# Ten rows of the last but one V tile, loaded by GpSimd on chosen DMA engines

## Chip, cores and metric

The kernel runs on one core of a Trainium2 chip. The metric is device time in microseconds (us): the median over the runs shown, and for the profile the span of one profiled execution. The core has five engines: TensorE (PE in the profile, its weight loads PEld), VectorE (DVE), ScalarE (ACT), GpSimd (POOL) and SyncE (SP). Data comes from the chip's memory (HBM) into the on-chip SBUF through 16 DMA engines that work beside them.

## What is computed

One decode step: attention of a single query over a cache of 65,536 keys and values for 8 key/value heads (16 query heads, head size 256), and a small gated feed-forward block, mixed by a sigmoid gate.

```
x = A_x                                        # 1 x 448
g = sigmoid((x * gate_w).sum(-1))
q = (x @ wq) as 16 heads of 256
scores = q . k_cache * 256**-0.5               # 8 kv heads x 65536 x 256, bf16
p = softmax(scores)
a = (p . v_cache) as 1 x 4096, then @ wo
gate, up = B_x @ W_gate, B_x @ W_up            # 448 x 1792 each
b = (relu(gate) * up) @ W_down
out = g * a + (1 - g) * b
```

The K and V caches are 268 MB each in bf16 and every byte of them is read once.

## The kernel before

**Tiles.** A K or V cache of a head is cut into four tiles, 32 K tiles and 32 V tiles in all. A tile is 128 partitions of 128 rows (U = 128) of 256 bf16 values: 64 KB in each partition, 8 MB in all. Three such buffers exist in SBUF, `ring[0]` to `ring[2]`. V tile 30 is the last but one (NT - 2 in the code, NT = 32), and it goes into `ring[1]`. V tile 31 is loaded in three pieces, `PIECES` = rows 0 to 64, 64 to 112 and 112 to 128, into `ring[2]`.

**Partitions of a V tile.** `v_src(n)` views a tile in memory as 32 groups of 4 partitions. Group p stands in partitions 4p to 4p + 3 of the buffer, so groups 16 to 31 are partitions 64 to 127.

**Order of the loads.** All large loads are issued by SP in the order of the list `order` (L381 to L394): K and V tiles by turns, then V tiles 28 to 31, then the output weights `wo` in six pieces of falling size (`WO`). A load waits until the last reader of its buffer has finished: for V tile 30 that reader is the product with V tile 28 (`free(("v", 30))`). What SP has issued waits in a queue at the DMA engines and is worked off in order.

**The work on a V tile.** `make_pv` writes two kinds of operation. ACT first copies the probabilities of the tile into `pcur` (L591), and this copy waits for the tile's load; only V tile 31 has the wait on its matmuls instead. Then 64 matmuls (L584) add the product to the accumulator `O`. After V tile 31, DVE scales the accumulator (L607 and L610), PE gathers it (L557), DVE copies it to `attnA` (L789), and 64 matmuls with `wo` (L551) follow, piece by piece as `wo` lands. Two casts (L796 and L797) and a store (L798) end the kernel.

**Numbers of a plan.** Each operation has a key, a planned time, and stands in its engine's program in the order of the keys; what it waits for is semaphores (`emit`, L89). A DMA adds 16 to its semaphore, and an operation that depends on several DMAs of one semaphore waits for their total.

**GpSimd** makes a few constants at the start (L443 to L461) and issues no load.

Of the kernel before, what the change touches and what calls it, by code (L numbers as in the profile page):

```python
# [27 lines left out]
class _Plan:  # L28
# [14 lines left out]
    def dma(self, eng, key, sem, fn, deps=()):  # L43
        if sem not in self.dsem:
            self.dsem[sem] = self.es.enter_context(self.nc.semaphore("d_" + sem))
        o = _Op(eng, key, fn, deps, dma=sem)
        self.ops.append(o)
        return o
# [212 lines left out]
def bass_gated_mix__gqa_block_cached__glu_gated_reglu__decode_kernel(  # L261
# [15 lines left out]
    DH = A_k_cache.shape[3]  # L277
# [4 lines left out]
    U = 128  # L282
    TK = 128 * U
    NTH = S // TK
    NT = H * NTH
# [11 lines left out]
    with es:  # L297
# [3 lines left out]
        ring = [sb("ring%d" % i, [128, U * DH], BF) for i in range(NRING)]  # L301
# [3 lines left out]
        scr = sb("scr", [128, 1024], BF)  # L305
        xcur = sb("xcur", [128, 136], BF)
        xm = sb("xm", [128, H * 128 + 8], BF)
# [63 lines left out]
        op, dma = pl.op, pl.dma  # L371
# [17 lines left out]
        for i, (lo, hi) in enumerate(PIECES):  # L389
            order.append(("vp", i, TILE * (hi - lo) / U))  # L390

        WO = [(0, 11), (11, 18), (18, 23), (23, 27), (27, 30), (30, 32)]
        for i, (lo, hi) in enumerate(WO):
            order.append(("wo", i, 0.27 * (hi - lo)))  # L394
        t = 3.0
        tL, issue = {}, []
# [16 lines left out]
        for kind, i, _ in order:  # L413
            if kind in ("k", "v") or (kind, i) in (("wo", 0), ("vp", 0)):
                r = place(kind, i)
# [105 lines left out]
        def v_src(i):  # L521
            h, a = divmod(i, NTH)
            return A_v_cache[0, h, :, :].rearrange("(t g p u) d -> g p t (u d)", t=NTH, g=NTH, u=U)[a]
# [37 lines left out]
        l_, qk, smax, aexp, pv, pc, last, first = {}, {}, {}, {}, {}, {}, {}, {}  # L561
        pending = []

        def free(key):
            out_ = []
            for f in freed[key]:
                out_.append(l_[f] if isinstance(f, str) else qk[f[1], 1] if f[0] == "k" else pv[f[1]])
            return out_
# [6 lines left out]
        def make_pv(n, lo, hi, sl, tv, dep):  # L575
            h, a = divmod(n, NTH)

            def f_pv(lo, hi):
                return lambda e: f_mm(e, lo, hi)

            def f_mm(e, lo, hi):
                for k in range(lo // 2, hi // 2):
                    g = k % 4
                    ins = e.matmul(OP[32 * g:32 * g + 4, :], pcur[a % 2][:, 4 * k:4 * k + 4],  # L584
                                   ring[sl][:, k * 512:(k + 1) * 512],
                                   start=False, stop=False, skip_group_check=True,
                                   tile_position=(0, 32 * g))
                return ins
            tp = max(tv, last["tev", h])
            if lo == 0:  # L590
                pc[n] = op("ap", max(tp - 5, last["tev", h] - 0.5), lambda e: e.copy(  # L591
                    pcur[a % 2][:].rearrange("p (k i) -> p k i", i=4),
                    ptp[:].rearrange("p (k i f) -> p k i f", i=4, f=4)[:, :, :, a]), last["ev", h] + [pv.get(n - 2)])
            if lo == 0 and a == 0:
                zero_o(last["tev", h] - 0.3, h)
            if n < NT - 1:
                pc[n].deps.append(dep)
            deps = ([dep] if n == NT - 1 else []) + [pc[n]] + ([last["zo", h]] if a == 0 and lo == 0 else [])
            if n >= NT - NTH and a == 1:
                for q_, (l2, h2) in enumerate(PIECES):  # L600
                    pv[n] = op("pv", tp + 0.1 * q_, f_pv(l2, h2), deps if q_ == 0 else [pc[n]], tag=("tail", 1, q_))
            else:
                tag = ("pv", a % 2, sl) if n < NT - NTH else ("tail", a % 2, 0 if n < NT - 1 else [q_[0] for q_ in PIECES].index(lo))
                pv[n] = op("pv", tp, f_pv(lo, hi), deps, tag=tag)
            if a == NTH - 1 and hi == U:
                tn = last["T", h + 1] + 18.5 if n < NT - 1 else tp + 1.2
                o1 = op("dx", tn, lambda e: e.tensor_scalar(o_sb[:], OP[:, 0:256], rcm[:, 0:1], None, ALU.mult),  # L607
                        [pv[n], last.get(("otr", h - 1)), last["rc", h]])
                last["ocp", h] = o1
                o1 = op("dx", tn + 0.05, lambda e: e.scalar_tensor_tensor(  # L610
                    o_sb[:], OP[:, 256:512], rcm[:, 1:2], o_sb[:], ALU.mult, ALU.add), [o1, last.get(("ec", h))])

                if h < H - 1:
                    o2 = op("pv", tn + 0.3, lambda e: f_sel(e, lambda d_: ecur[:, 7 - d_:135 - d_]),
                            [o1], tag="otr")
                else:
                    o2 = op("pv", tn + 0.5, lambda e: f_sel(e, lambda d_: esel[:, 120 - 16 * h - d_:248 - 16 * h - d_]),
                            [o1, g_es, l_["axz"]])
                if h < H - 1:
                    last["l5", h + 1].deps.append(o1)  # L620
                last["o1", h], last["otr", h] = o1, o2
                last["tn", h] = tn + 1

        for kind, i, t in sorted(issue, key=lambda q: q[0] != "wq"):
# [51 lines left out]
            elif kind == "k":  # L676
                n = i
                h, t_ = divmod(n, NTH)
                sl = slot["k", n]
# [28 lines left out]
                if t_ == NTH - 1:  # L708
# [18 lines left out]
                    for rd in range(2):  # L727
# [10 lines left out]
                        p = op("pe", tt + 0.5, f_ptr, [rsc, g_idb], tag=("ptr", rd))  # L738
# [29 lines left out]
            elif kind in ("v", "vp"):  # L768
                if kind == "v":
                    n, lo, hi = i, 0, U  # L770
                    sl = slot["v", n]
                    dep = dma("sp", t, "r%d" % sl, lambda e, sl=sl, n=n: e.dma_start(ring[sl][:], v_src(n)), free(("v", n)))
                else:
                    n, (lo, hi) = NT - 1, PIECES[i]
                    sl = slot["vp", 0]
                    dep = dma("sp", t, ("wq", "wqh", "wd")[i], lambda e, sl=sl, n=n, lo=lo, hi=hi: e.dma_start(  # L776
                        ring[sl][:, lo * 256:hi * 256], v_src(n)[:, :, lo * 256:hi * 256]), free(("vp", 0)))
                args = (n, lo, hi, sl, tL[kind, i], dep)
                if ("tev", n // NTH) in last:
                    make_pv(*args)  # L780
                else:
                    pending.append(args)
            elif kind == "wo":
                lo, hi = WO[i]
                l_["wo", i] = dma("sp", t, "wo%d" % i, lambda e, lo=lo, hi=hi: e.dma_start(  # L785
                    wo_sb[:, lo:hi, :], A_wo.rearrange("(p s) n -> p s n", s=32)[:, lo:hi, :]), free(("wo", 0)))

        LAST = last["tn", H - 1]
        aA = op("dx", LAST + 0.3, lambda e: e.tensor_copy(attnA[:], AX_ps), [last["otr", H - 1]])  # L789
        for i, (lo, hi) in enumerate(WO):  # L790
            def f_wo(e, lo=lo, hi=hi):
# [84 lines left out]
```

## Time and profile before

| what | before |
|---|---|
| device time, median of 3 runs | 1275.81 us (1275.78 to 1275.91) |
| span of the profiled execution | 1274.3 us |
| bytes read | 549.03 MB |
| PE busy | 365.9 us (29%) |
| DVE busy | 630.1 us (49%) |
| ACT busy | 78.0 us (6%) |
| POOL busy | 4.6 us (0%) |

The span runs from the first to the last instruction of the profiled execution. The device time has 1.5 us more in it. The profile has a page with the busy time of each engine, the DMA queues and the chain of work that ended last, and views that answer questions on the trace: a timeline of instructions, groups by line, busy time and DMA share in chosen stretches. Times in them are us from the start of the span.

### The profile page before, as it was taken

To read this page: it belongs to the slowest core of one execution; us is meant where nothing else is said; L and a number is where in the kernel's file an instruction comes from. 1 tells how busy PE (TensorE), PEld (TensorE's weight loads), DVE (VectorE), ACT (ScalarE), POOL (GpSimd) and SP (SyncE) were. 2 spreads that over 40 slices of the span, in tenths; PEclk is the share of its full clock that TensorE was granted. 3 is DMA by queue.
4 is the path that set the end of the run, shared out by engine and by line. 5 is a ranking of instruction groups with operands and counts; after the bars stand their busy time and mean duration, and the time that the engine had idled before them with its cause. 6 is when DMAs were issued, how large, how long until landed. Compare 5 with 4: busy or idle time off the path is not lost.

```text
span 1274.3 us, 10240 instructions
## 1 busy us (share of the span) xinstructions
PE 365.9 (29%) x4497; PEld 151.4 (12%) x4505; DVE 630.1 (49%) x309; ACT 78.0 (6%) x163; POOL 4.6 (0%) x23
## 2 busy tenths in 40 slices
PE   0534321133320332312233222323302332112525
PEld 0101110011110111101111110111100111001201
DVE  4777655553455633557433565335654355553300
ACT  0001100010000100001000010000000010000100
POOL 1000000000000000000000000000000000000000
PEclk9766665666655666656666656666566666566667
DMA  9999999999999999999999999999999999999998
GB/s 411 430 436 432 426 430 434 432 443 432 430 432 432 434 442 430 430 434 430 438 438 430 430 434 430 440 438 428 430 434 430 444 434 428 430 436 430 442 421 369
DMA packets 11389, 549.13 MB, mean 431 GB/s; under 512 B 1267, under 2 KB 1654, under 8 KB 2294
## 3 DMA queue, kind: packets, MB, share of 16 engines
q1 hardware_dynamic: 11378, 549.03, 99.7%
q8 instruction: 4, 0.07, 0.0%
q14 instruction: 3, 0.02, 0.0%
q10 hardware_dynamic: 4, 0.00, 0.0%
HBM read 549.03 MB, written 0.00 MB: 431 GB/s over the span
## 4 chain that ended last, share of the span: by engine, by line
DMA 81%; PE 16%; DVE 2%; ACT 1%; issue 1%; SPq 0%; ACTq 0%
DMA ring<-in_A_v_cache_dram 74%; PE O L584 13%; DMA ring<-in_A_wo_dram 3%; DMA ring<-in_A_wq_dram 2%; DMA ring<-in_A_k_cache_dram 2%; DVE ring L529 1%; PE ST L540 1%; ACT pcur L591 1%; PE O L501 1%; PE A_ps L551 0%; SPq L785 0%; SPq L776 0%; PE O L653 0%; DVE ring L660 0%; PE A_ps L653 0%
## 5 line engine op out<-in xcount | busy, mean ns | idle before, releaser
L529 DVE STREAM_TRANSPOSE ring<-ring 128x4096 uint32<-128x4096 uint32 x128 | 557.6, 4413 | 196.9 <-DMA ring<-in_A_k_cache_dram 196.9
L584 PE MATMUL O<-ring,pcur 128*4 128x512 bf16 x2048 | 187.3, 545 | 790.4 <-ACT pcur L591 781.9
L703 DVE TENSOR_REDUCE nmb<-ST 128x1 f32<-128x512 f32 x32 | 22.1, 692 | 345.9 <-PE ST L540 345.9
L584 PEld LDWEIGHTS O<-ring,pcur 128*4 128x4 bf16 x2048 | 59.3, 111 | 914.8 <-ACT pcur L591 794.6
L540 PE MATMUL ST<-ring,xcur 128*16 128x512 bf16 x2048 | 136.7, 420 | 44.3 <-DVE ring L529 43.7
L540 PEld LDWEIGHTS ST<-ring,xcur 128*16 128x16 bf16 x2048 | 62.4, 92 | 112.1 <-DVE ring L529 48.6
L705 ACT ACTIVATE P_sb<-ST,nmb 128x512 bf16<-128x512 f32 x32 | 44.6, 1392 | 368.3 <-DVE nmb L703 368.3
L591 ACT COPY pcur<-ptp 128x256 bf16<-128x256 bf16 x32 | 13.2, 415 | 732.6 <-DMA ring<-in_A_v_cache_dram 732.6
L607 DVE TENSOR_SCALAR o_sb<-O,rcm 128x256 bf16<-128x256 f32 x8 | 3.8, 479 | 61.1 <-PE O L584 61.1
L730 DVE TENSOR_TENSOR P_sb<-P_sb,hs 128x1024 bf16<-128x1024 bf16 x16 | 18.9, 1222 | 8.1 <-ACT hs L724 8.1
L735 PE MATMUL PT<-identb,P_sb 128*128 128x128 bf16 x128 | 14.5, 282 | 17.6 <-DVE P_sb L730 17.3
L501 PE MATMUL O<-ring,P_sb 128*128 128x512 bf16 x28 | 8.5, 477 | 17.3 <-DMA ring<-in_A_wq_dram 17.3
L735 PEld LDWEIGHTS PT<-identb,P_sb 128*128 128x128 bf16 x128 | 10.7, 127 | 19.9 <-DVE P_sb L730 19.9
L744 ACT COPY ptp<-PT 128x256 bf16<-128x256 bf16 x32 | 10.3, 375 | 23.0 <-PE PT L735 23.0
L705 ACT ACTIVATION_READ_ACCUMULATOR P_sb<-ST,nmb 128x1 f32 x32 | 8.3, 258 | 0.0
L501 PEld LDWEIGHTS O<-ring,P_sb 128*128 128x128 bf16 x28 | 3.2, 117 | 22.2 <-issue 20.5
L551 PE MATMUL A_ps<-ring,attnA 128*1 128x224 bf16 x64 | 5.3, 322 | 1.1 <-DMA ring<-in_A_wo_dram 1.0
L719 PE MATMUL M_ps<-identf,hs 128*2 128x128 f32 x8 | 2.3, 283 | 10.0 <-DVE hs L717 10.0
L756 DVE RECIPROCAL rc<-M_ps 128x2 f32<-128x2 f32 x8 | 1.4, 171 | 7.5 <-PE M_ps L755 7.5
L755 PE MATMUL M_ps<-hs,ones_f 128*128 128x2 f32 x16 | 4.5, 352 | 0.0
L722 PE MATMUL M_ps<-mx,nselT 2*128 2x1 f32 x16 | 3.2, 268 | 3.0 <-DVE mx L721 3.0
L755 PEld LDWEIGHTS M_ps<-hs,ones_f 128*128 128x128 f32 x16 | 4.0, 311 | 0.0
(93 smaller groups left out, 68.6 us busy)
## 6 DMA issues: line engine op xcount, KB each, us to landing
ring<-in_A_v_cache_dram SPq DMA_DIRECT2D x1, 4096.0 KB, 22.1
ring<-in_A_wq_dram SPq DMA_DIRECT2D x1, 3072.0 KB, 28.9
ring<-in_A_v_cache_dram SPq DMA_DIRECT2D x1, 3072.0 KB, 28.8
ring<-in_B_W_down_dram SPq DMA_DIRECT2D x1, 1568.0 KB, 53.0
ring<-in_B_W_gate_dram SPq DMA_DIRECT2D x1, 1344.0 KB, 26.3
ring<-in_B_W_up_dram SPq DMA_DIRECT2D x1, 1344.0 KB, 29.2
ring<-in_A_wo_dram SPq DMA_DIRECT2D x1, 1232.0 KB, 33.0
ring<-in_A_v_cache_dram SPq DMA_DIRECT2D x1, 1024.0 KB, 30.7
```

The costliest lines, as they stand in the source:

```text
L501: ins = e.matmul(QN_ps, xw3[:, kt, 31 - m:159 - m], rhs, start=(kt == 0 and m == 0), stop=(kt == R3 and m == J // 4 - 1))
L529: return lambda e: e.transpose(v, v)
L540: ins = e.matmul(bank[32 * w:32 * w + 16, :], xcur[:, x0:x0 + 16], ktv[sl][:, u0:u0 + 16, c, :, r_], start=(b == 0 and c == 0 and r_ == 0) ...
L551: ins = e.matmul(A_ps[32 * g:32 * g + 1, 0:D2], lhsT, rhs[:, g * D2:(g + 1) * D2], start=start, stop=stop, skip_group_check=True, tile_pos ...
L584: ins = e.matmul(OP[32 * g:32 * g + 4, :], pcur[a % 2][:, 4 * k:4 * k + 4], ring[sl][:, k * 512:(k + 1) * 512], start=False, stop=False, s ...
L591: pc[n] = op("ap", max(tp - 5, last["tev", h] - 0.5), lambda e: e.copy(pcur[a % 2][:].rearrange("p (k i) -> p k i", i=4), ptp[:].rearrange ...
L703: smax[n] = op("dv", sx, lambda e, n=n, t_=t_: e.tensor_reduce(NM[:, t_:t_ + 1], ST[n % 2][:], AX.X, ALU.max, negate=True), [qk[n, 1], las ...
L705: aexp[n] = op("ac", sx + 1, lambda e, n=n, t_=t_: e.activation(P_sb[:, t_:2048:4], ST[n % 2][:], ACTF.Exp, bias=NM[:, t_:t_ + 1], scale=1 ...
L730: rsc = op("dv", tt, lambda e, pb=pb: e.tensor_tensor(pb, pb, X[:, 12:16].unsqueeze(1).to_broadcast([128, 256, 4]), ALU.mult), [h7, aexp[n]])
L735: ins = e.transpose(PT[rd][:, s * 128:(s + 1) * 128], P_sb[:, (rd * 8 + s) * 128:(rd * 8 + s + 1) * 128], identb[:, :])
L744: ins = e.copy(dst, src)
L755: l3 = mop("pe", T + 19, lambda e: e.matmul(LS_ps, ones_f[:, :], X[:, 6:8], start=True, stop=True), [l2, c_one], tag="l3")
```

## The change

SP loads V tile 30 without part of it: first rows 0 to 117 of all 128 partitions, then rows 118 to 127 (`UW` = 10 rows) of partitions 0 to 63. The ten rows of partitions 64 to 127 are loaded by GpSimd. The table `WINDOWS` lists eight transfers, each as a flag and a number of groups. Four of them carry the tile's data, 3, 6, 2 and 5 groups of 4 partitions, 16 groups in all. Between them and after the last stand four tiny loads of 4, 2, 7 and 3 rows with two pieces of 64 bytes each, from `B_W_gate` into the scratch tile `scr`, whose content nobody reads afterwards. The eight numbers add up to 32, twice the number of DMA engines. All eight use the semaphore `vw`. ACT's copy for V tile 30 waits for `vw` as well, which is why a list of dependencies takes the place of the single one in `make_pv`.

```diff
+        UW = 10
+        WINDOWS = [(0, 3), (1, 4), (0, 6), (1, 2), (0, 2), (1, 7), (0, 5), (1, 3)]
...
-                pc[n].deps.append(dep)
-            deps = ([dep] if n == NT - 1 else []) + [pc[n]] + ([last["zo", h]] if a == 0 and lo == 0 else [])
+                pc[n].deps.extend(dep)
+            deps = (dep if n == NT - 1 else []) + [pc[n]] + ([last["zo", h]] if a == 0 and lo == 0 else [])
...
-                    dep = dma("sp", t, "r%d" % sl, lambda e, sl=sl, n=n: e.dma_start(ring[sl][:], v_src(n)), free(("v", n)))
+                    if n == NT - 2:
+                        part = lambda sl, n, p0, p1, u0, u1: dict(
+                            out=ring[sl][4 * p0:4 * p1, u0 * DH:u1 * DH], in_=v_src(n)[p0:p1, :, u0 * DH:u1 * DH])
+                        us = U - UW
+                        dma("sp", t, "r%d" % sl, lambda e, sl=sl, n=n: e.dma_start(**part(sl, n, 0, 32, 0, us)), free(("v", n)))
+                        dep = dma("sp", t + 0.01, "r%d" % sl, lambda e, sl=sl, n=n: e.dma_start(**part(sl, n, 0, 16, us, U)), free(("v", n)))
+                        p0 = 16
+                        for j, (skip, k) in enumerate(WINDOWS):
+                            if skip:
+                                seg = lambda a: a.rearrange("p (s w) -> p s w", s=2)[:, :, 0:32]
+                                sw = dma("gp", t + 0.02 + 0.01 * j, "vw", lambda e, k=k, j=j: e.dma_start(
+                                    seg(scr[16 * j:16 * j + k, 0:320]), seg(B_W_gate[0:k, 0:320])), [l_["xm"]] + free(("v", n)))
+                            else:
+                                sw = dma("gp", t + 0.02 + 0.01 * j, "vw", lambda e, sl=sl, n=n, p0=p0, k=k: e.dma_start(
+                                    **part(sl, n, p0, p0 + k, us, U)), free(("v", n)))
+                                p0 += k
+                        assert p0 == 32
+                    else:
+                        dep = dma("sp", t, "r%d" % sl, lambda e, sl=sl, n=n: e.dma_start(ring[sl][:], v_src(n)), free(("v", n)))
...
-                args = (n, lo, hi, sl, tL[kind, i], dep)
+                args = (n, lo, hi, sl, tL[kind, i], [dep] + ([sw] if (kind, i) == ("v", NT - 2) else []))
```

SP's program near its end before the change, with the semaphores that a load waits for in brackets. The two loads with `s_pe` are V tiles 28 and 29, the next is V tile 30, then come the three pieces of V tile 31 and the first two of `wo`:

```order
L772 DMA ring<-in_A_v_cache_dram 128x1x32768 [waits s_pe] x2
L772 DMA ring<-in_A_v_cache_dram 128x1x32768 [waits s_pv]
L776 DMA ring<-in_A_v_cache_dram 128x1x16384 [waits s_pv]
L776 DMA ring<-in_A_v_cache_dram 128x1x12288
L776 DMA ring<-in_A_v_cache_dram 128x1x4096
L785 DMA ring<-in_A_wo_dram 128x4928
L785 DMA ring<-in_A_wo_dram 128x3136
```

And with the change:

```order
L792 DMA ring<-in_A_v_cache_dram 128x1x32768 [waits s_pe] x2
L778 DMA ring<-in_A_v_cache_dram 128x1x30208 [waits s_pv]
L779 DMA ring<-in_A_v_cache_dram 64x1x2560
L796 DMA ring<-in_A_v_cache_dram 128x1x16384 [waits s_pv]
L796 DMA ring<-in_A_v_cache_dram 128x1x12288
L796 DMA ring<-in_A_v_cache_dram 128x1x4096
L805 DMA ring<-in_A_wo_dram 128x4928
L805 DMA ring<-in_A_wo_dram 128x3136
```

V tile 30 is now two loads of SP in the place of one; the order of all others is the same.

GpSimd's program with the change, from its last two constants to its end. Before, the branch at the end followed the constants:

```order
L462 TENSOR_SCALAR selc<-selc 128x2 [waits s_gp]
L463 TENSOR_SCALAR selc<-selc 128x2 [waits s_gp]
L787 DMA ring<-in_A_v_cache_dram 12x1x2560 [waits s_pv]
L784 DMA scr<-in_B_W_gate_dram 4x2x32 [waits s_dx]
L787 DMA ring<-in_A_v_cache_dram 24x1x2560
L784 DMA scr<-in_B_W_gate_dram 2x2x32
L787 DMA ring<-in_A_v_cache_dram 8x1x2560
L784 DMA scr<-in_B_W_gate_dram 7x2x32
L787 DMA ring<-in_A_v_cache_dram 20x1x2560
L784 DMA scr<-in_B_W_gate_dram 3x2x32
L828 UNCONDITIONAL_BRANCH
```

Eight loads are added, the first of them behind the same wait that V tile 30 has on SP.

ACT's program at its end with the change. The four copies at L593 are those of V tiles 28 to 31:

```order
L593 COPY pcur<-ptp 128x256 [waits d_r1,s_pv,s_ac]
L593 COPY pcur<-ptp 128x256 [waits d_r2,s_pv]
L593 COPY pcur<-ptp 128x256 [waits d_vw,d_r1,s_pv]
L593 COPY pcur<-ptp 128x256 [waits s_pv]
L817 CAST P_sb<-A_ps 1x224 [waits s_pv]
```

Only the third row differs: the copy for V tile 30 waits for `d_vw` too. The programs of PE and DVE are the same as before.

## The prediction

> **What bounds the kernel now.** I read the page first: the DMA lines, the queues and the chain that ended last.
>
> ```profile
> DMA  9999999999999999999999999999999999999998
> ...
> q1 hardware_dynamic: 11378, 549.03, 99.7%
> q8 instruction: 4, 0.07, 0.0%
> q14 instruction: 3, 0.02, 0.0%
> q10 hardware_dynamic: 4, 0.00, 0.0%
> HBM read 549.03 MB, written 0.00 MB: 431 GB/s over the span
> ...
> DMA 81%; PE 16%; DVE 2%; ACT 1%; issue 1%; SPq 0%; ACTq 0%
> ```
>
> SP's queue q1 keeps the 16 DMA engines busy for 99.7% of the span. So the transfers bound the kernel, the large loads are spread evenly, and one engine moves 431 / 16 = 26.9 GB/s. A change that moves no fewer bytes can only act on the last engine to finish, so I read the chain in order of time at its end, and the busy time in quarters of a us there.
>
> ```profile
> 1236.40 35.84 DMA ring<-in_A_wo_dram
> 1272.24 0.04 issue
> 1272.28 0.38 PE A_ps L551 x4
> 1272.66 0.02 issue
> 1272.68 0.38 DVE P_sb L796
> ```
>
> ```profile
> core 0: us, PE busy (x) PEld busy (x) DVE busy (x) ACT busy (x) POOL busy (x), PEclk, DMA share, GB/s
> 1268.00:1270.00 2.00, 1.54 (x18) 0.87 (x20) 0.00 (x0) 0.00 (x0) 0.00 (x0) 0.60 1.01 406
> 1270.00:1270.25 0.25, 0.25 (x6) 0.19 (x4) 0.00 (x0) 0.00 (x0) 0.00 (x0) 0.50 0.70 272
> 1270.25:1270.50 0.25, 0.25 (x6) 0.15 (x4) 0.00 (x0) 0.00 (x0) 0.00 (x0) 0.50 0.55 215
> 1270.50:1270.75 0.25, 0.25 (x6) 0.00 (x0) 0.00 (x0) 0.00 (x0) 0.00 (x0) 0.50 0.44 172
> 1270.75:1271.00 0.25, 0.25 (x4) 0.09 (x4) 0.00 (x0) 0.00 (x0) 0.00 (x0) 0.50 0.42 165
> 1271.00:1271.25 0.25, 0.25 (x6) 0.15 (x4) 0.00 (x0) 0.00 (x0) 0.00 (x0) 0.50 0.29 111
> 1271.25:1271.50 0.25, 0.25 (x6) 0.11 (x2) 0.00 (x0) 0.00 (x0) 0.00 (x0) 0.50 0.34 129
> 1271.50:1271.75 0.25, 0.25 (x6) 0.01 (x4) 0.00 (x0) 0.00 (x0) 0.00 (x0) 0.50 0.18 65
> 1271.75:1272.00 0.25, 0.25 (x8) 0.17 (x6) 0.00 (x0) 0.00 (x0) 0.00 (x0) 0.89 0.02 7
> ```
>
> The last number but one is the share of the 16 engines that are busy. Up to 1270.0 all work. Then they fall out one by one: 0.30 x 16 = 4.8 idle in the first quarter, 7.2 in the second, and from 1271.0 to 1271.5 a plateau of 0.29 to 0.34, which is five engines, before the last stops near 1271.8. The end waits for the late five or six of 16. What is left after 1270.0 is (0.70 + 0.55 + 0.44 + 0.42 + 0.29 + 0.34 + 0.18 + 0.02) x 0.25 = 0.735 us per engine: shared out evenly it would end at 1270.74. **No change of placing alone can gain more than 1271.8 - 1270.7 = 1.1 us**, 0.09% of the time.
>
> **The change part by part.** *Bytes per engine.* Ten rows of a group of 4 partitions are 4 x 10 x 512 = 20,480 bytes; at 26.9 GB/s that is a unit of 0.76 us on one engine. The ten rows of the whole tile are 32 units, two for each engine before. Now SP loads the lower 16, one for each engine, and GpSimd the upper 16. I take it, as the change's own words and the sum of 32 suggest, that a transfer of k groups uses k engines in a row and the next begins behind them. The table then covers, loaded and skipped by turns, engines 0-2, (3-6), 7-12, (13-14), 15-0, (1-7), 8-12, (13-15). Engines 0 and 8 to 12 get two units from GpSimd, 1, 2, 7 and 15 one, and 3, 4, 5, 6, 13 and 14 none. Against before, six engines carry one unit more, four the same, six one unit less. The Trainium skill, "DMA: Bandwidth & Descriptors", section "Why a DMA increments its semaphore by 16 and not by 1", states this rule of a cursor for GpSimd's transfers, and beside it an exception that is priced as a rival below.
>
> *Which engines are late* no row says, since none names an engine. What the rows give is the number: six are relieved, and five to six are late. The sum takes it that they are the same ones.
>
> *Small packets.* The four pieces of SP's second load and GpSimd's rows are packets of their own, the tiny loads add up to four pieces on a relieved engine, and I let every engine report each of the nine added transfers: some 17 more packets on a relieved engine, 21 on the others. The view of the DMA queues from 1269 to 1273 has packets of that kind:
>
> ```profile
> DMA packets 324, 0.68 MB, mean 169 GB/s; under 512 B 46, under 2 KB 174, under 8 KB 324
> ...
> q1 hardware_dynamic: 324, 0.68, 43.1%
> ```
>
> 0.431 x 16 x 4 us / 324 = 85 ns for a packet of 0.68 MB / 324 = 2.1 KB, whose bytes alone take 78 ns. So a packet costs between 7 ns beyond its bytes and 85 ns in all. Most of the added ones carry next to nothing, so I take 7 ns: 17 x 7 = 0.12 us on a relieved engine, 0.15 us on the others; at 85 ns they would cost 1.4 us and eat the gain.
>
> *The sum.* Late engines: -0.76 + 0.12 = -0.64, so 1271.8 becomes 1271.16. Engines with a unit more gain 0.76 + 0.15 = 0.91 and stay ahead of that if they ended by 1270.25, where the rows have 4.8 to 7.2 idle: six just fit. I take 0.6 us off. The work behind the last landing, 0.38 + 0.38 us and the store, follows unchanged; all pieces of `wo` move together, since each waits for the same late engines.
>
> *GpSimd's queue.* Its program ended early, so nothing of its own is delayed by the wait for V tile 28:
>
> ```profile
> 6.45 0.19 POOL L461 TENSOR_SCALAR selc<-selc 128x2 f32<-128x2 f32 x1
> ```
>
> Who waits for it is ACT's copy for V tile 30, and the product behind it.
>
> ```profile
> 1211.78 0.53 SPq L772 DMA_DIRECT2D ring<-in_A_v_cache_dram  x1
> 1231.68 1.83 SPq L776 DMA_DIRECT2D ring<-in_A_v_cache_dram  x3
> 1233.55 8.72 SPq L785 DMA_DIRECT2D ring<-in_A_wo_dram  x6
> ```
>
> ```profile
> 1244.15 0.74 ACT L591 COPY pcur<-ptp 128x256 bf16<-128x256 bf16 x2 [18.94 <-DMA ring<-in_A_v_cache_dram]
> ...
> 1244.62 5.23 PE L584 MATMUL O<-ring,pcur 128*4 128x512 bf16 x64 [12.99 <-ACT pcur L591]
> 1253.91 2.82 PE L584 MATMUL O<-ring,pcur 128*4 128x512 bf16 x32 [4.07 <-DMA ring<-in_A_v_cache_dram]
> 1261.13 3.58 PE L584 MATMUL O<-ring,pcur 128*4 128x512 bf16 x32 [4.40 <-DMA ring<-in_A_v_cache_dram]
> ```
>
> The loads go out at 1211.78 and the copy starts at 1244.15: 32.4 us of cover. Behind it PE idles 4.07 and 4.40 us before the pieces of V tile 31, so GpSimd's last row may land 32.4 + 8.5 = 40.9 us after the release before anything ends later. The trace has no load issued by GpSimd; the nearest rows are SP's: three in 1.83 us, 0.6 each, and `wo`'s six in 8.72, the mean 1.45. Eight at 0.6 to 1.45 take 5 to 12 us, far inside the cover, and cost nothing. SP's own extra issue, some 0.6 us at 1212.3, stands before its wait until 1231.68.
>
> *V tile 29.* GpSimd's rows go in while that tile is still moving and can hold it up by two units, 1.5 us, on six engines that are ahead of the late ones. Even in full that would move SP's issue at 1231.68 to 1233.2, with V tile 30 in the queue until 1244: nothing.
>
> *First use.* What GpSimd's first load costs at the start or outside the span no row shows. I bound it by 0 and by the 1275.81 - 1274.3 = 1.5 us that now lie outside the span, and take 0, since it would have to delay SP's stream. By the same difference the span of 1274.3 becomes 1273.7 and the median 1275.81 becomes **1275.2 us**.
>
> **The rivals.** (a) *The heavier engines include a late one.* For it: no row ties an engine to its lateness, and the seven packets of instructions on q8 and q14, 0.09 MB in all, some 0.5 us each, may fall on other engines in another program. Against: the numbers match. Price +0.91: 1276.7. (b) *A late engine is among the four that keep their load.* Five late engines could be relieved and the sixth not. Price 0.15 us of packets: 1276.0. (c) *GpSimd's rows are spread from engine 0 on, partition by partition.* Transfers of 12, 24, 8 and 20 partitions would put 1 + 2 + 1 + 2 rows of 5,120 bytes, 0.19 us each, on engines 0 to 7, where four rows lay before: +0.38, and 0.15 of packets, 1276.3 if a late engine is among them. Against it: the tiny loads would then do nothing. The skill's section named above has this as its exception: some copies of GpSimd put the partitions, divided by 16 and rounded up, on each engine from the first on. (d) *GpSimd is too slow, and its wait takes the place of the landing.* It is on ACT's copy for V tile 30 and decides from 40.9 us on. The longest issue in the trace:
>
> ```profile
> L785 SPq DMA_DIRECT2D ring<-in_A_wo_dram x6: 331/433/5869, 1233.5 to 1236.4; - x6
> ```
>
> Eight of 5.87 us are 47 us, 6 us past the cover: 1281.8, slower. Against it: that issue is one behind eight others in a full queue, and the median is 0.43. The Trainium skill, "SBUF — State Buffer", section "SBUF: two separate sides", warns that VectorE can lock GpSimd out while it writes a load's descriptors. By its 3.1 us for a load so blocked, eight take 25 us, an estimate still inside the cover, and VectorE's row
>
> ```profile
> 1264.77 0.48 DVE L607 TENSOR_SCALAR o_sb<-O,rcm 128x256 bf16<-128x256 f32 x1 [61.06 <-PE O L584]
> ```
>
> shows it idle for 61.06 us before 1264.77, all of that stretch.
>
> **How the numbers follow.** Forecast 0.56, (a) 0.15, (b) 0.17, (c) 0.06, (d) 0.04, and 0.02 for a gain whose cause I don't see. The range goes from the even end, 1275.81 - 1.1 = 1274.7, to 1276.8, which takes in (a) to (c) and the bounds of the first use and of the packets (-0.64 to +0.7); only (d) and the unseen gain lie outside. The forecast alone is 1274.9 to 1275.6. A measurement of this kernel tells about 0.2% from no change, 2.55 us: forecast, (a), (b) and (c) all lie within it, 0.94 together; slower is (d), 0.04; faster 0.02.
>
> **What would show it.** Right: the same packets' view shows a third data queue with 0.33 MB; the last `wo` piece lands near 1271.6 and the share after 1270.0 falls without the plateau of five; ACT's copy for V tile 30 stays near 1244 with a landing of SP's as its releaser. A plateau kept at its place speaks for (b), a last landing near 1273.1 for (a), a new releaser of that copy by GpSimd's load for (d). Wrong altogether: a shift of the stream before 1211, or more than 1.1 us gained at the end.

## The result, and the profile after

The changed kernel takes 1279.89 us, the median of six runs (1279.46 to 1280.59). The kernel before, run beside it, takes 1275.86 us (1275.77 to 1275.98). The ratio is 1.0032, with a 95% interval of 1.0021 to 1.0043: the change costs 4.0 us, where the forecast had 0.6 us gained. In the profiled executions the span grew from 1274.3 to 1278.8 us, 4.5 us; the profiled one of the changed kernel, 1280.59 us, is the longest of its six.

The page of the changed kernel, its DMA line, its queues (packets, MB, share of the 16 engines' time) and the shares of its chain:

```profile
DMA  9999999999999999999999999999999999999998
...
q1 hardware_dynamic: 11458, 548.71, 99.7%
q0 software_dynamic: 448, 0.33, 0.1%
...
DMA 81%; PE 15%; DVE 2%; ACT 1%; SPq 1%; issue 1%; ACTq 0%
```

The new queue q0 is GpSimd's, with the 0.33 MB that the change moved to it. The transfers still bound the kernel, and the DMA engines still read as fully busy. The chain of waits of the changed kernel, in order of time at its end, has the same last links as before:

```profile
1242.13 34.56 DMA ring<-in_A_wo_dram
1276.68 0.04 issue
1276.73 0.38 PE A_ps L553 x4
1277.10 0.02 issue
1277.12 0.38 DVE P_sb L816
```

The last piece of `wo` lands at 1276.68 where it landed at 1272.24: 4.44 us, all but 0.1 us of what the span grew. So the stream of transfers as a whole is late, and nothing behind it. Its end in half-microseconds, from the changed kernel's busy time by windows (the last number but one is the share of the 16 DMA engines that are busy, the last one GB/s):

```profile
1274.00:1274.50 0.50, 0.21 (x6) 0.20 (x8) 0.00 (x0) 0.00 (x0) 0.00 (x0) 1.00 0.96 378
1274.50:1275.00 0.50, 0.43 (x10) 0.15 (x4) 0.00 (x0) 0.00 (x0) 0.00 (x0) 1.00 0.81 315
1275.00:1275.50 0.50, 0.12 (x4) 0.12 (x6) 0.00 (x0) 0.00 (x0) 0.00 (x0) 1.00 0.43 167
1275.50:1276.00 0.50, 0.42 (x8) 0.15 (x4) 0.00 (x0) 0.00 (x0) 0.00 (x0) 1.00 0.16 59
1276.00:1276.50 0.50, 0.33 (x6) 0.17 (x6) 0.00 (x0) 0.00 (x0) 0.00 (x0) 1.00 0.03 11
```

What is left after 1274.0 is (0.96 + 0.81 + 0.43 + 0.16 + 0.03) x 0.5 = 1.2 us for each engine, so an even end would have been at 1275.2, against 1270.74 before. The even end moved by 4.5 us, and the last landing by as much. The engines are therefore about as uneven as they were: the mean engine is late, not one of them. Where it became late is seen in the stretches of the last V tiles. Before:

```profile
1215.00:1230.00 15.00, 4.73 (x48) 1.58 (x52) 0.00 (x0) 0.41 (x1) 0.00 (x0) 0.50 1.05 455
1230.00:1240.00 10.00, 1.63 (x24) 0.42 (x16) 0.00 (x0) 0.00 (x0) 0.00 (x0) 0.67 1.01 433
1240.00:1250.00 10.00, 5.23 (x64) 1.70 (x64) 0.00 (x0) 0.74 (x2) 0.00 (x0) 0.60 0.90 387
1250.00:1260.00 10.00, 2.82 (x32) 0.85 (x32) 0.00 (x0) 0.00 (x0) 0.00 (x0) 0.74 0.98 418
```

And after:

```profile
1215.00:1230.00 15.00, 3.65 (x36) 1.22 (x40) 0.00 (x0) 0.41 (x1) 2.10 (x4) 0.57 1.03 425
1230.00:1240.00 10.00, 2.20 (x32) 0.65 (x24) 0.00 (x0) 0.00 (x0) 0.00 (x0) 0.67 0.98 379
1240.00:1250.00 10.00, 0.00 (x0) 0.00 (x0) 0.00 (x0) 0.00 (x0) 0.00 (x0) 0.50 0.99 350
1250.00:1260.00 10.00, 0.71 (x8) 0.24 (x12) 0.00 (x0) 0.74 (x2) 0.00 (x0) 0.50 0.98 378
```

The engines are busy in both, but they move fewer bytes: 15 x 30 + 10 x 54 + 10 x 37 + 10 x 40 GB/s x us = 1.76 MB are missing by 1260, which at 431 GB/s is 4.1 us. A share of busy time near 1 with a falling rate is what to look at here: the transfers became slower, not fewer.

The second thing to read is GpSimd's queue. GpSimd's loads in the changed kernel, by line (durations of the issue in ns as shortest, median and longest, then the landing):

```profile
L787 POOL DMA_DIRECT2D ring<-in_A_v_cache_dram x4: 590/602/769, 1212.3 to 1216.0; - x4
...
DMA to landing us min/median/max: 14.9/31.8/41.3
```

```profile
L784 POOL DMA_DIRECT2D scr<-in_B_W_gate_dram x4: 563/574/611, 1213.1 to 1216.5; - x4
...
DMA to landing us min/median/max: 18.9/33.3/42.2
```

The eight issues take 0.56 to 0.77 us each and are over by 1217.1. Yet the rows (L787) land 14.9 to 41.3 us after they were issued, and the tiny loads (L784) 18.9 to 42.2 us. The timeline of the changed kernel shows who waits for them:

```profile
1258.82 0.74 ACT L593 COPY pcur<-ptp 128x256 bf16<-128x256 bf16 x2 [32.52 <-DMA scr<-in_B_W_gate_dram]
```

ACT's copy for V tile 30 starts at 1258.82 instead of 1244.15, released by the last of GpSimd's tiny loads. So there are two suspects: a slower stream, and this new wait.

### The profile page after: what moved, and what is told of

Read it like the earlier page. It is cut to its first block, busy times and chain, and to the rows that moved or that the text cites. A ratio compares the mean times of both kernels' runs of the same rounds, so it can differ in the third digit from the quotient of the medians.

```text
span 1278.8 us, 10249 instructions
## 1 busy us (share of the span) xinstructions
PE 358.1 (28%) x4497; PEld 148.3 (12%) x4505; DVE 630.1 (49%) x309; ACT 78.0 (6%) x163; POOL 9.4 (1%) x31
## 4 chain that ended last, share of the span: by engine, by line
DMA 81%; PE 15%; DVE 2%; ACT 1%; SPq 1%; issue 1%; ACTq 0%
DMA ring<-in_A_v_cache_dram 74%; PE O L586 13%; DMA ring<-in_A_wo_dram 3%; DMA ring<-in_A_wq_dram 2%; DMA ring<-in_A_k_cache_dram 2%; DVE ring L531 1%; PE ST L542 1%; ACT pcur L593 1%; PE O L503 1%; SPq L805 1%; PE A_ps L553 0%; SPq L796 0%; PE O L655 0%; DVE ring L662 0%; PE A_ps L655 0%
## 5 line engine op out<-in xcount | busy, mean ns | idle before, releaser
L586 PE MATMUL O<-ring,pcur 128*4 128x512 bf16 x2048 | 180.9, 531 | 800.5 <-ACT pcur L593 800.5
L593 ACT COPY pcur<-ptp 128x256 bf16<-128x256 bf16 x32 | 13.2, 415 | 750.4 <-DMA ring<-in_A_v_cache_dram 717.9
L732 DVE TENSOR_TENSOR P_sb<-P_sb,hs 128x1024 bf16<-128x1024 bf16 x16 | 18.9, 1222 | 8.1 <-ACT hs L726 8.1
L787 POOL DMA_DIRECT2D ring<-in_A_v_cache_dram x4 | 2.6, 641 | 1205.7 <-PE O L586 1205.7
```

The lines of the kernel that those rows point to most:

```text
L732: rsc = op("dv", tt, lambda e, pb=pb: e.tensor_tensor(pb, pb, X[:, 12:16].unsqueeze(1).to_broadcast([128, 256, 4]), ALU.mult), [h7, aexp[n]])
```

## The experiments

"Before" in what follows is the kernel before, run beside each experiment. It took 1276.05, 1275.90, 1275.98 and 1275.93 us in the four groups of runs, and losses are against the one of the same group. Each diff is against the changed kernel, if nothing else is said; the dots stand for lines left out, and lines are cut at their ends where the rest is as before.

**The same loads, with nobody waiting.** GpSimd's rows go to a part of `ring[0]` that is not read again, and ACT's copy no longer waits for `vw`:

```diff
-  **part(sl, n, p0, p0 + k, us, U)), free(("v", n)))
+  out=ring[0][4 * p0:4 * (p0 + k), 20480:23040], in_=part(sl, n, p0, p0 + k, us, U)["in_"]), free(("v", n)))
...
-  args = (n, lo, hi, sl, tL[kind, i], [dep] + ([sw] if (kind, i) == ("v", NT - 2) else []))
+  args = (n, lo, hi, sl, tL[kind, i], [dep])
```

> All eight GpSimd loads stay, with the same shapes and bytes, but the four with V rows write into a part of ring[0] that nobody reads, and ACT's copy for V tile 30 does not wait for them. What is left out: the product with V tile 30 takes rows 118 to 127 of partitions 64 to 127 from what V tile 28 left there. Stream theory (each packet on GpSimd's queue takes about 0.16 us of a DMA engine's time: 4.5 us x 16 engines / 448 packets; the stream itself ends later): 1280 us, ACT's copy near 1247.5, last wo piece still near 1276.7. Wait theory (the landing of GpSimd's rows near 1258.8 holds up ACT's copy and with it PE): 1275.9 us, last wo piece near 1272.2.

Measured: 1279.79 us, ratio 1.0028 (1.0017 to 1.0039), a loss of 3.7 us. Its timeline has the copy released by SP's load again:

```profile
1246.78 0.74 ACT L593 COPY pcur<-ptp 128x256 bf16<-128x256 bf16 x2 [21.07 <-DMA ring<-in_A_v_cache_dram]
```

and in its chain the last piece of `wo` still lands late:

```profile
1241.54 34.27 DMA ring<-in_A_wo_dram
1275.81 0.04 issue
```

The copy is 12 us earlier than in the changed kernel and nearly the whole loss stays. The stream is slow by itself; the wait is not what sets the end.

**The wait without GpSimd.** The kernel before, with V tile 31 in four pieces and ACT's copy for V tile 30 held until the second of them has landed:

```diff
-        PIECES = [(0, 64), (64, 112), (112, 128)]
+        PIECES = [(0, 64), (64, 96), (96, 112), (112, 128)]
...
-                    dep = dma("sp", t, ("wq", "wqh", "wd")[i], ...
+                    dep = dma("sp", tL["v", NT - 2] - 18.9 + 0.1 * i, ("wq", "r0", "wqh", "wd")[i], ...
...
+                    if i == 1:
+                        pc[NT - 2].deps.append(dep)
```

This diff is against the kernel before. The loads of the pieces also get another planned time, and the second piece the semaphore `r0`.

> The kernel before, without any GpSimd load, in which ACT's copy for V tile 30 waits as late as in the changed kernel: V tile 31 comes in four pieces instead of three, and the copy waits for the second of them, which lands near 1258.7. Wait theory: the whole loss is here, 1279.9 us. Stream theory: the loads end where they did (last wo piece near 1272.2), and the wait alone costs less, since wo has landed when PE comes to it: PE ends its 128 products near 1269.2 and needs 64 x 55 ns = 3.5 us behind 1271.0, so 1277.8 us at most.

Measured: 1277.17 us, ratio 1.0009 (0.9999 to 1.0018), a loss of 1.1 us with an interval that just reaches no loss. Its chain no longer ends with a landing:

```profile
1258.57 0.42 ACT pcur L591
...
1270.19 3.25 PE A_ps L551 x64
1273.44 0.02 issue
1273.46 0.38 DVE P_sb L798
```

From the copy to the cast are 14.9 us of work without a gap. So a copy at 1258.8 puts the cast at about 1273.7. That is later than the 1272.68 of before, but 3.4 us earlier than the 1277.12 of the changed kernel: the wait would cost about a microsecond, and in the changed kernel it is hidden behind the late stream.

**One transfer of GpSimd's in the place of eight.**

```diff
-        WINDOWS = [(0, 3), (1, 4), (0, 6), (1, 2), (0, 2), (1, 7), (0, 5), (1, 3)]
+        WINDOWS = [(0, 16)]
```

> GpSimd loads the same 16 groups in one transfer, with no tiny loads; ACT's copy waits for it. Every engine carries what it did before. Stream theory: 64 packets of rows and an eighth of the 384 small ones, 112 instead of 448, so a quarter of the loss: 1277.0 us. The landing comes after 7 packets per engine that take turns with packets of 2.4 us, near 1231. Wait theory: it lands before 1244, no loss, 1275.9 us.

Measured: 1278.97 us, ratio 1.0024 (1.0014 to 1.0033), a loss of 2.9 us. Its queue q0 has 80 packets in the place of 448, and its landing comes 15.5 us after the issue. With a price for each packet most of the loss would have gone with the packets, to 1277.0 us; it did not.

**Small packets of SP.** In the run just told, the records of GpSimd's 80 packets, five for each engine on the mean, stretch over 11.2 us (1216.5 to 1227.6), 4.6 times the 2.42 us of one of SP's packets of 64 KB. So they seem to take turns with these. Here SP loads V tiles 29 and 30 in pieces of 16 rows, so that its packets are 8 KB:

```diff
-  dma("sp", t, "r%d" % sl, lambda e, sl=sl, n=n: e.dma_start(**part(sl, n, 0, 32, 0, us)), free(("v", n)))
+  cut = list(range(0, us, 16)) + [us]
+  for c_, (ua, ub) in enumerate(zip(cut, cut[1:])):
+      dma("sp", t + 0.001 * c_, "r%d" % sl, lambda e, sl=sl, n=n, ua=ua, ub=ub: e.dma_start(**part(sl, n, 0, 32, ua, ub)), free(("v", n)))
...
+                    elif n == NT - 3:
+                        for c_ in range(8):
+                            dep = dma("sp", t + 0.001 * c_, "r%d" % sl, lambda e, sl=sl, n=n, c_=c_: e.dma_start(
+                                ring[sl][:, c_ * 4096:(c_ + 1) * 4096], v_src(n)[:, :, c_ * 4096:(c_ + 1) * 4096]), free(("v", n)))
```

> The changed kernel, but SP loads V tiles 29 and 30 in pieces of 16 rows, so that its packets beside GpSimd's are 8 KB (0.30 us) and not 64 KB (2.42 us). If GpSimd's packets take turns with SP's one for one, its 28 packets per engine land in 28 x 0.46 = 13 us, near 1230, and ACT's copy for V tile 30 is released by SP's own load. Wait theory: 1275.9 us. Stream theory with a fixed price per packet: 1280 us all the same.

Measured: 1280.52 us, ratio 1.0034 (1.0022 to 1.0047), a loss of 4.5 us. GpSimd's packets are through by about 1228 in this kernel, and ACT's copy starts at 1248.90, released by SP's load. So the long packets explain when GpSimd's rows land, but not the loss. What the small pieces cost without GpSimd was not tried. The 8 KB packets of before took 0.3135 us each, 0.011 more than the pace of the 64 KB packets gives; by that the 1,920 new ones cost about 1.3 us for each engine, an estimate, so part of the 4.5 us is theirs.

**No GpSimd at all.** SP loads what the change splits: rows 0 to 117 of all partitions, ten rows of partitions 0 to 63, then ten of 64 to 127:

```diff
-  p0 = 16
-  for j, (skip, k) in enumerate(WINDOWS):
...
+  dep = dma("sp", t + 0.02, "r%d" % sl, lambda e, sl=sl, n=n: e.dma_start(**part(sl, n, 16, 32, us, U)), free(("v", n)))
```

> No load by GpSimd at all. SP loads rows 0 to 117 of V tile 30 on all 128 partitions, then the ten rows of partitions 0 to 63 and the ten of partitions 64 to 127, each by all 16 engines. Crowding theory (a transfer that lets all 16 engines write into half of the partitions slows them and those beside them, whoever issues it): about 1.4 us for each half, as the stretch from 1240 to 1250 of the run with one GpSimd transfer lost, where SP's half was written: 1278.8 us. Queue theory (two queues at work on one DMA engine cost time): no second queue, 1276.0 us.

Measured: 1278.29 us, ratio 1.0018 (1.0008 to 1.0028), a loss of 2.4 us with no second queue, no tiny load and no new wait. Its control loads the ten rows of all 128 partitions at once, as packets of the same 5,120 bytes (the diff is against the kernel with the halves):

```diff
-  dep = dma("sp", t + 0.01, "r%d" % sl, lambda e, sl=sl, n=n: e.dma_start(**part(sl, n, 0, 16, us, U)), free(("v", n)))
-  dep = dma("sp", t + 0.02, "r%d" % sl, lambda e, sl=sl, n=n: e.dma_start(**part(sl, n, 16, 32, us, U)), free(("v", n)))
+  dep = dma("sp", t + 0.01, "r%d" % sl, lambda e, sl=sl, n=n: e.dma_start(**part(sl, n, 0, 32, us, U)), free(("v", n)))
```

> No load by GpSimd. SP loads rows 0 to 117 and then the ten rows of all 128 partitions in one load, so that the packets are as small as in the split by halves (5 KB), but each engine writes the partitions that it writes anyway. Crowding theory: 1276.0 us. Queue theory: 1276.0 us. If the small packets themselves cost, as much is lost as with the halves: 1278.8 us.

Measured: 1275.92 us, ratio 1.0000 (0.9990 to 1.0010): nothing lost. The windows in which the ten rows arrive, with the ten rows in halves:

```profile
1240.00:1242.00 2.00, 0.00 (x0) 0.00 (x0) 0.00 (x0) 0.00 (x0) 0.00 (x0) 0.50 0.62 159
1242.00:1244.00 2.00, 0.00 (x0) 0.00 (x0) 0.00 (x0) 0.00 (x0) 0.00 (x0) 0.50 1.12 287
1244.00:1246.00 2.00, 0.00 (x0) 0.00 (x0) 0.00 (x0) 0.00 (x0) 0.00 (x0) 0.50 0.93 306
```

and over all partitions:

```profile
1240.00:1242.00 2.00, 0.00 (x0) 0.00 (x0) 0.00 (x0) 0.00 (x0) 0.00 (x0) 0.50 0.94 384
1242.00:1244.00 2.00, 0.00 (x0) 0.00 (x0) 0.00 (x0) 0.14 (x1) 0.00 (x0) 0.50 1.02 435
1244.00:1246.00 2.00, 1.67 (x19) 0.53 (x21) 0.00 (x0) 0.60 (x2) 0.00 (x0) 0.50 1.06 459
```

The rates differ by 225, 148 and 153 GB/s. Over 2 us each that is 1.05 MB, or 2.4 us at 431 GB/s: about all of the loss falls into these 6 us, in which the halves arrive.

**The second queue alone.** GpSimd loads five rows of all 128 partitions in one transfer, the same 0.33 MB (`UW` = 5, and no second load of SP's):

```diff
-        UW = 10
-        WINDOWS = [(0, 3), (1, 4), (0, 6), (1, 2), (0, 2), (1, 7), (0, 5), (1, 3)]
+        UW = 5
+        WINDOWS = [(0, 32)]
...
-                        p0 = 16
+                        p0 = 0
```

> GpSimd loads five rows of all 128 partitions in one transfer, as many bytes as before in its queue, SP the other 123 rows in one load. Every engine keeps its partitions. Crowding theory: 1276.0 us. Queue theory: what the run with one GpSimd transfer lost between 1215 and 1230, 1.4 us or more, since there are twice as many packets: 1277.4 us or more.

Measured: 1276.02 us, ratio 1.0001 (0.9991 to 1.0010): nothing lost. The queues of that kernel between 1217 and 1259, and its copy:

```profile
q0 software_dynamic: 76, 0.31, 1.8%
```

```profile
1243.98 0.74 ACT L593 COPY pcur<-ptp 128x256 bf16<-128x256 bf16 x2 [18.18 <-DMA ring<-in_A_v_cache_dram]
```

GpSimd's queue costs nothing here, where its transfer covers all partitions, and its rows are in time. By the records its 64 packets of 5,120 bytes take 0.200 us each, and SP's packets beside them keep their pace (2.33 us for 62,976 bytes, as 2.42 for 65,536).

**The tiny loads alone, and the transfers without them.** The first has V tile 30 loaded by SP as before, and GpSimd issues the four tiny loads only; the second leaves them out of the change:

```diff
-        WINDOWS = [(0, 3), (1, 4), (0, 6), (1, 2), (0, 2), (1, 7), (0, 5), (1, 3)]
+        WINDOWS = [(1, 4), (1, 2), (1, 7), (1, 3)]
...
+                        dep = dma("sp", t, "r%d" % sl, lambda e, sl=sl, n=n: e.dma_start(**part(sl, n, 0, 32, 0, U)), free(("v", n)))
```

> SP loads the whole of V tile 30 as before the change; GpSimd issues the four tiny loads alone, and ACT's copy waits for them. Crowding theory: they move 2 KB in all, 1276.0 us. Queue theory with a price per packet: the tiny loads and their share of the small packets are some 190 of 448 packets, 1277.7 us.

```diff
-        WINDOWS = [(0, 3), (1, 4), (0, 6), (1, 2), (0, 2), (1, 7), (0, 5), (1, 3)]
+        WINDOWS = [(0, 3), (0, 6), (0, 2), (0, 5)]
```

> The changed kernel without the tiny loads: GpSimd's four transfers of 3, 6, 2 and 5 groups follow one another, so each of the 16 engines should get one group, as in the single transfer. The changed kernel lost 1 us more than the one with the single transfer (1278.97). If that is the uneven load on the engines, it is gone here: 1279.0 us. If it is the cutting in four transfers of few engines, it stays: 1279.8 us. The tiny loads by themselves cost nothing.

Measured: 1276.03 us for the tiny loads alone, ratio 1.0000 (0.9991 to 1.0010), so by themselves they cost nothing that can be told from the noise. Without them 1279.35 us, ratio 1.0026 (1.0016 to 1.0036), a loss of 3.4 us, between one transfer (2.9) and the change (4.0). The steps of 0.5 and 0.6 us are inside the intervals, so what the cutting and the tiny loads add to each other stays open.

**Without SP's half.** The change with SP's second load taken out, so that rows 118 to 127 of partitions 0 to 63 aren't loaded:

```diff
-  dma("sp", t, "r%d" % sl, lambda e, sl=sl, n=n: e.dma_start(**part(sl, n, 0, 32, 0, us)), free(("v", n)))
-  dep = dma("sp", t + 0.01, "r%d" % sl, lambda e, sl=sl, n=n: e.dma_start(**part(sl, n, 0, 16, us, U)), free(("v", n)))
+  dep = dma("sp", t, "r%d" % sl, lambda e, sl=sl, n=n: e.dma_start(**part(sl, n, 0, 32, 0, us)), free(("v", n)))
```

> The changed kernel without SP's second load: rows 118 to 127 of partitions 0 to 63 of V tile 30 are left out and keep what V tile 28 left there. 0.33 MB less is 0.76 us. Crowding theory, each half a price of its own: SP's half goes with its 1.2 us (half of what the two halves on SP cost), 1279.9 - 1.2 - 0.8 = 1277.9 us. If GpSimd's part alone is the loss: 1279.9 - 0.8 = 1279.1 us. If SP's half is all of it: 1275.2 us.

Measured: 1279.76 us, ratio 1.0030 (1.0018 to 1.0041). It seems to say that SP's half costs nothing, but its chain tells otherwise:

```profile
1261.42 0.02 issue
1261.44 0.04 ACTq L95
1261.47 0.04 issue
1261.52 0.43 ACT pcur L593
...
1272.79 3.25 PE A_ps L553 x64
1276.04 0.02 issue
1276.06 0.38 DVE P_sb L815
```

Here the 64 matmuls with `wo` run without a gap: each piece of `wo` was there when its turn came, and what ends last is ACT's copy, released at 1261.5 by GpSimd's last load. The stream became shorter, the landing on q0 came 2.7 us later than in the change, and the wait took the place of the stream. So the time of this run doesn't price SP's half. It shows that the wait is the next bound behind the stream. The end of its stream does give the prices: the last piece of `wo`, issued at 1235.3, landed 39.1 us later, at 1274.4, where it landed at 1272.24 before, although 0.33 MB, 0.76 us, were left out. GpSimd's loads alone thus made the stream about 2.9 us late, and of the 4.44 us of the changed kernel about 1.5 are left for SP's half. Both are estimates from one profiled execution each.

**By the byte?** The two halves of SP with twenty rows in the place of ten (no load by GpSimd, as in the run with ten):

```diff
-        UW = 10
+        UW = 20
```

> The two halves on SP, no load by GpSimd, with 20 rows in the place of ten, so twice the bytes in loads of 64 partitions. If crowding costs by the byte, the loss doubles: 1275.9 + 2 x 2.4 = 1280.7 us. If it is a price for a change from one kind of load to the other, it stays at 1278.3 us.

Measured: 1280.29 us, ratio 1.0033 (1.0021 to 1.0046), a loss of 4.3 us against 2.4 for ten rows. The loss grows with the bytes in the halves, 1.1 to 1.2 us for each 0.33 MB, as a rate does and a price for each transfer doesn't.

**Where it is crowded.** Three runs ask whether it is the partitions that are written or the memory that is read. No load is by GpSimd, and the diffs show what takes the place of SP's halves. The first reads half the groups at a time, but writes every second partition of all 128:

```diff
+  for q in range(4):
+      dep = dma("sp", t + 0.01 + 0.01 * q, "r%d" % sl, lambda e, sl=sl, n=n, q=q: e.dma_start(
+          out=ring[sl][q % 2:128:2, (us + 5 * (q // 2)) * DH:(us + 5 * (q // 2) + 5) * DH],
+          in_=v_src(n)[16 * (q // 2):16 * (q // 2) + 16, :, (us + 5 * (q % 2)) * DH:(us + 5 * (q % 2) + 5) * DH]), free(("v", n)))
```

> No load by GpSimd. SP loads the ten rows of V tile 30 in four loads of 64 rows of 2,560 bytes. Each load reads from one half of the groups, as the halves did, but writes every second of all 128 partitions, so that the 16 engines stay spread over them. The values of the ten rows stand in other partitions than they should, and the product with them is not the reference's. Crowding at the destination: 1276.0 us. Crowding at the source, in memory: 1278.3 us, as with the halves.

Measured: 1278.05 us, ratio 1.0016 (1.0007 to 1.0026), a loss of 2.1 us. By its expectation that speaks for the source. But its loads still write 64 partitions each, and which engine carries which row no record names, so it left both possible. The second keeps the halves of SP's run and reads the ten rows from one unbroken block:

```diff
-  dep = dma("sp", t + 0.01, "r%d" % sl, lambda e, sl=sl, n=n: e.dma_start(**part(sl, n, 0, 16, us, U)), free(("v", n)))
+  dep = dma("sp", t + 0.01, "r%d" % sl, lambda e, sl=sl, n=n: e.dma_start(out=ring[sl][0:64, us * DH:U * DH], in_=A_k_cache[0, 0, 0:640, :].rearrange('(p u) d -> p (u d)', u=10)), free(("v", n)))
...
```

> SP loads V tile 30 as in the kernel that lost 2.4 us (rows 0 to 117 of all partitions, then ten rows of partitions 0 to 63, then of 64 to 127), but the ten rows are read from one unbroken block of the K cache, 64 pieces of 5,120 bytes that follow each other, 0.33 MB for each load. The values of these ten rows are therefore not V's. If the crowding is in the partitions that are written: 1278.3 again, 2.4 over before. If it is in the memory that is read, where V's half rows lie 64 KB or more apart: 1276.0.

The third reads 64 rows of a tile at a time and writes all 128 partitions in their usual order:

```diff
-  dep = dma("sp", t + 0.01, "r%d" % sl, lambda e, sl=sl, n=n: e.dma_start(**part(sl, n, 0, 16, us, U)), free(("v", n)))
+  dep = dma("sp", t + 0.01, "r%d" % sl, lambda e, sl=sl, n=n: e.dma_start(out=ring[sl][:, (us + 0) * DH:(us + 5) * DH], in_=k_src(0)[0:64, us * DH:U * DH]), free(("v", n)))
...
```

In both, a second load of the same kind follows for the other 64 rows.

> SP loads rows 0 to 117 of V tile 30, then five rows' worth of all 128 partitions from the ten last rows of partitions 0 to 63 of the first K tile (64 stretches of 5,120 bytes, 64 KB apart, two pieces of 2,560 bytes each), then five from those of 64 to 127. The source is a half at a time, the destination all partitions in their usual order. The values of these ten rows are therefore not V's. If the crowding is in the partitions that are written: 1276.0. If it is in the memory that is read: 1278.

Measured: 1279.35 us for the unbroken source, ratio 1.0026 (1.0016 to 1.0036), and 1276.03 us for all partitions, ratio 1.0001 (0.9991 to 1.0011). The stretch in which the ten rows arrive, with the unbroken source:

```profile
1240.00:1242.00 2.00, 0.00 (x0) 0.00 (x0) 0.00 (x0) 0.00 (x0) 0.00 (x0) 0.50 0.60 120
1242.00:1244.00 2.00, 0.00 (x0) 0.00 (x0) 0.00 (x0) 0.00 (x0) 0.00 (x0) 0.50 1.32 286
1244.00:1246.00 2.00, 0.00 (x0) 0.00 (x0) 0.00 (x0) 0.00 (x0) 0.00 (x0) 0.50 0.95 247
```

and with half a source but all partitions:

```profile
1240.00:1242.00 2.00, 0.00 (x0) 0.00 (x0) 0.00 (x0) 0.00 (x0) 0.00 (x0) 0.50 0.59 233
1242.00:1244.00 2.00, 0.00 (x0) 0.00 (x0) 0.00 (x0) 0.00 (x0) 0.00 (x0) 0.50 1.26 521
1244.00:1246.00 2.00, 1.36 (x16) 0.51 (x20) 0.00 (x0) 0.74 (x2) 0.00 (x0) 0.50 0.95 410
```

The mean over the 6 us is 218 GB/s in the first and 388 in the second. Half a source loses nothing when each load writes all 128 partitions, and a smoother source didn't relieve the halves. So the crowding is on the side that is written. SP's loads that lose write 64 partitions each, 0 to 63, 64 to 127, or every second one, and GpSimd's write up to 64. That they lie together is therefore not what matters; why these cost and loads of 128 don't, no run here shows.

The records of the single packets of these loads, between 1212 and 1250, say the same. At the pace of the 64 KB packets of before (2.42 us for 65,536 bytes) 5,120 bytes take 0.19 us:

| SP's load of the last rows | packets | mean of one, us | at the pace of before, us | loss, us |
|---|---|---|---|---|
| ten rows, all partitions | 128 of 5,120 bytes | 0.202 | 0.189 | 0.0 |
| ten rows, all partitions, half the source | 256 of 2,560 bytes | 0.105 | 0.095 | 0.1 |
| ten rows, every second partition | 256 of 2,560 bytes | 0.165 | 0.095 | 2.1 |
| ten rows, in halves | 128 of 5,120 bytes | 0.320 | 0.189 | 2.4 |
| ten rows, in halves, unbroken source | 128 of 5,120 bytes | 0.390 | 0.189 | 3.4 |
| twenty rows, in halves | 128 of 10,240 bytes | 0.721 | 0.378 | 4.3 |

In the changed kernel the 64 packets of SP's half take 0.317 us, GpSimd's 64 only 0.229. The neighbours suffer more: the 60,416-byte packets of V tile 30 take 2.43 us where they take 2.24 beside whole loads, and the 32,768-byte packets of V tile 31 take 1.43 in the place of 1.22. What all packets after 1205 took beyond these paces, added up and divided by the 16 engines, is 0.6 us in the two halves themselves, 3.6 us in the packets of V tiles 29 to 31 beside them, and 0.3 us in packets under 1 KB: 4.5 us, as the last landing moved by 4.44. So most of the loss is not in the loads of 64 partitions but in the loads of all partitions that run beside them. With SP's halves alone the two parts are 0.9 and 1.2 us.

## Why the prediction was wrong

*The bound* held: the stream of transfers sets the end, and the links behind the last landing cost what they did. The limit of 1.1 us on any gain was not put to the test, since nothing was gained.

*Bytes per engine* is the step that failed. The prediction gave a unit of 20,480 bytes 0.76 us on one engine, whichever partitions it goes to and whatever moves beside it, and then only counted units. The rate of 26.9 GB/s behind that was read from loads of all 128 partitions, the only ones in that stretch. The change splits 0.65 MB into loads of 64 partitions. A unit is four packets, and those took 4 x 0.317 = 1.27 us in SP's half and 4 x 0.229 = 0.92 us in GpSimd's. Above all, they slowed the packets of the whole loads beside them, 3.6 us for each engine, which the prediction put at nothing without a row for it. SP's two halves alone lose 2.4 us, and the same rows over all partitions lose nothing. In the sum, a term was missing of 4.0 us by the medians and 4.4 by the profiled executions. By the ends of their streams about 2.9 us of it belong to GpSimd's loads and about 1.5 to SP's half, both estimates.

The prediction used the Trainium skill, "DMA: Bandwidth & Descriptors", for the rule of the cursor, and overlooked that page's section "Rules for kernel authors", which advises one transfer of 128 partitions in the place of two to disjoint halves. The trace agrees with the advice, 1278.29 against 1275.92 us, though the reason given there, that the halves share the same engines, would not make them slower than one whole load. A better reason is in "SBUF — State Buffer", section "Door 1: The DMA port swizzle (why `[64,N]` ≈ `[32,N]`)": the rate of a transfer depends on how many of 16 ports its partitions reach, and partitions 0 to 63 reach half of them. The factors on SP's packets agree, 1.6 (0.320 / 0.202) to 1.9 (0.721 / 0.378). GpSimd's packets, 1.15 (0.229 / 0.200), do not, and every second partition of all 128 reaches all 16 ports of that section's table and still loses 2.1 us. So the ports as the cause are argued and not shown: to test them one would have to know which engine carries which row.

*Which engines are late* could not be tested, since no record names an engine, and it decided nothing: the distance from the even end to the last one is about a microsecond before and after. The count of five late engines was itself rough, since windows with a share of 1.26 or 1.32 show that records of packets overlap. The gain of 0.64 and the prices of rivals (a) to (c), all of them counts of units, are thus neither borne out nor refuted; they are lost in a shift of 4 us.

*Small packets* were rightly priced at little, though there were more of them than counted: 448 on GpSimd's queue and 80 more on SP's, 33 for each engine in the place of 17 to 21. Those under 1 KB took about 0.3 us more for each engine than before, where the prediction had 0.12 to 0.15 us, and the tiny loads alone lose 0.1 us, inside the interval.

*GpSimd's queue* was half right. The issues cost 0.56 to 0.77 us, at the low end of the assumed 0.6 to 1.45. But the prediction took the end of the issues, 5 to 12 us, for the time of the rows, and never asked when they land behind SP's packets. The last of them landed 41.3 us after its issue. So rival (d), at 0.04, had the right place, and its sign was the one that came, but the wrong mechanism: ACT's copy got the new releaser, 46.5 us after the release at 1212.3, through waiting in the queue and not through slow issues. And the price was not paid: the chain and the run with nobody waiting show that the stream ended later still. The cover was also longer than the 40.9 us of the prediction. By the 14.9 us that follow the copy in the run with the wait alone, a copy at 1257.8 still meets the cast at 1272.68, 46 us after the release at 1211.78.

*First use* was taken as nothing, and the run in which GpSimd loads all partitions, 1276.02 us, bears it out. *V tile 29* was given up to 1.5 us on some engines without effect. Its copy (`pcur`) started at 1225.88 in the place of 1224.80, 1.1 us late, but as part of the slow stream, which did move the end.

The one sign named for "wrong altogether" that looks like this, more than 1.1 us, was named for gains alone; for a loss the list had no row that asks whether the rate stays at 431 GB/s while the change's transfers run. That was the question to ask.

## What to carry to other kernels

In a kernel bound by its DMA stream, a transfer that covers 64 of the 128 partitions isn't a free unit that can be put where it suits: it slows the loads beside it, and they can pay more than it does. Cut a tile by columns and not by partitions. Price a new transfer from rows of the same shape, and where there is none, say that the rate is unknown and put a slower stream into the range, for as long as the new transfers are under way. A load that is issued cheaply on a second queue can still land tens of microseconds later behind long packets of the first one, so the cover to compare with is that of the landing.

## What the hardware showed that was not expected

Three things. SP's loads of 64 partitions took 1.6 to 1.9 times as long for a packet and slowed the packets beside them, by the byte: 2.4 us for ten rows, 4.3 for twenty. GpSimd's, spread over 39 us, were hardly slower themselves, 0.229 us in the place of 0.200, and still cost the stream about 2.9 us through their neighbours. Reading from an unbroken block, which should be the easier source, lost more and not less in the same halves, 3.4 us (1278.92 to 1279.57) beside 2.4 (1277.96 to 1278.51); why stays open. And GpSimd's eight small loads needed 448 packets, of which 64 carry the rows, and took up to 42 us to land beside SP's 64 KB packets, where one load with 80 packets needed 14.5 (128 partitions) or 15.5 (64).
